# Attention, gated feed-forward and expert layer on one core: the loads of the first tiles as single steps, other tile groups, and the last block's columns split 384 and 128

## The chip, the cores and the metric

The kernel runs on one core of one Trainium2 chip. A core has five engines with an instruction stream each: TensorE (PE in the rows, with its weight loads as PEld) multiplies matrices into PSUM, VectorE (DVE), ScalarE (ACT) and GpSimd (POOL) work element by element, and SyncE (SP) issues most DMAs. The metric is the device time of one execution in microseconds, as the median of several runs. It is lower when the work ends sooner.

## The reference

```python
def _attn_ref(q, k, v):                       # q, k, v: (4, 8, 576, 64)
    scores = scale * np.matmul(q, k.transpose(0, 1, 3, 2))
    gamma = 1.0 - 2.0 ** (-5.0 - np.arange(H))
    Dmat = np.where(rel >= 0, gamma[:, None, None] ** rel, 0.0)
    return np.matmul(scores * Dmat, v)

def _moe_ref(x, w_gate, w_val, w_out, rms_g):  # x: (2304, 512), inner width 1536
    xn = x / np.sqrt(np.mean(x * x, axis=-1, keepdims=True) + 1e-06) * rms_g
    g = xn @ w_gate
    return (g / (1.0 + np.exp(-g)) * (xn @ w_val)) @ w_out

def _moe2_ref(x, w_gate, w_output_gate, w1, w2):  # 8 experts, inner width 1024
    e_idx = np.argmax(x @ w_gate, axis=1)
    ...
    for e in range(E):
        h = np.maximum(x[mask] @ w1[e], 0.0)
        out[mask] = gate_w[mask, None] * eom[mask, e, None] * (h @ w2[e])
```

The three layers follow each other: attention with decay, then a gated feed-forward layer, then one expert for each token.

## The kernel before

The 2304 tokens are 18 tiles of 128 (`TILES`, L67): tiles 0 to 3 are the first 128 positions of the four batches, and so on; tiles 16 and 17 hold two half tiles each. Float32 operands are split into a high and a low float16 half, and a product is three float16 matmuls. Attention runs tile by tile with a state per batch (`z`), in steps that have one letter each: `l` loads, `s` splits, `c` makes the scores, `o` the output with its norm, `z` the state. The four tiles of `FIRST` do it in float32: their transposed q and k come ready from memory (`qk_t`), the scores go through PSUM, are multiplied on DVE by the decay `dmat` into a tile `pp`, and `pa` is the output. From `pa` the norm goes ACT (`junk`, the sum of squares), DVE (`ss`), POOL (`rr`), DVE (`xh`), four PE transposes (`tp`), and ACT and DVE write `xt`, the input of the next layer.

The feed-forward layer takes the tiles in groups (`GROUPS`, L70: 4, 3, 3, 3, 3 and 2 tiles). For each of 12 slices `ft` of the inner width, `moe_h` (L822) makes `hg` and `hv` in PSUM (12 matmuls each, as wide as the group, in two PSUM buffers), ACT and DVE turn them into `th`, and ACT and POOL into `uh` and `ul`; `moe_out` (L854) adds their product with `wo` into an accumulator `o` for each tile. While a group is in this layer, attention of the next group's tiles runs in between. The weights come in 18 pieces of 1 MB (`load_piece`, `conv_piece`) that ACT, DVE and POOL have to decode and split (`st`, `du`, `gv_h`, `gv_l`, `wo_h`, `wo_l`); all of that lies in the first stage.

After each group `route` finds each token's expert and scatters its row. Tiles from `LATE` on go to a table of their own (80 rows for expert 0), so that expert 0 can begin with the earlier ones. `exp_l1` makes an expert's hidden layer, `exp_l2t` or `exp_l2` its output; the results go back by `yr`, an addition on POOL, a multiplication on ACT and a scattered DMA from POOL. The last expert writes by rows, and its last block of 128 tokens goes through `exp_last` (L1171).

The order on the engines isn't the order of the code. `Plan` records every operation (all show as line 232 or 294), gives each a cost (`_cost`, L328) and a due time, and a list scheduler (`schedule`, L355) writes the streams. What is recorded when in the first stage is the string `START` (L88): one word for each step, `d` loads a weight piece, `k` decodes it, `h` and `y` are pieces of `moe_h` and `moe_out`, `f` loads `dmat`, `g` loads `gain`. Until the first `moe_h` the scheduler fills every time in which its own model has TensorE idle with a matmul of zeros (`busy<-warm`, 256 columns), which computes nothing:

```python
if first in end and end[first] <= t and self.filled not in start and free.get("PE", 0.0) <= t:
    o = Op("PE", us, -1, 0)
```

How many such matmuls stand in the stream is fixed when the kernel is built. SP issues its DMAs in stream order, and a DMA that reuses one of eight semaphores waits for the one eight before it.

Of the kernel before, what the change touches and what calls it, by code (L numbers as in the profile page):

```python
# [10 lines left out]
F16 = mybir.dt.float16  # L11
# [22 lines left out]
LATE = 16  # L34
# [43 lines left out]
IN_R = 2  # L78
# [10 lines left out]
l1 d1 d0 l0 d3 s1 s0 f c1 k1 l2 k0 g c0 d12 d13 o1 o0 h0-1-0-1 k12 h0-1-1-2 h1-2-0-2 z1 s2 k3 c2 o2 e4 d2 d5 z2 k2 m  # L89
l4 d7 d8 y0-0-2 k13 z0 l3 s3 k5 h0-1-2-3 h3-4-0-2 y0-2-3 k7 c3 h1-2-2-3 h2-3-0-3 k8 s4 d4 h3-4-2-3 d6 o3 y2-1-2 k4  # L90
y3-1-3 y2-0-1 k6 d14 h2-3-3-4 h0-2-3-4 d9 y1-0-3 y2-2-3 h7-8-3-4 l5 z3 y3-0-1 h5-6-0-3 d16 k14 d15 h7-8-0-3 h4-5-0-3
y5-0-3 d10 y4-0-2 k9 e3 k15 h6-7-0-2 k16 k10 e1 c4 h6-7-2-3 d11 h8-9-3-4 o4 y4-2-3 s5 y6-2-3 e7 y6-1-2 h6-7-3-4 c5
y7-0-3 h8-10-0-3 h3-4-3-4 o5 e6 k11 h9-10-3-4 y6-0-1 l6 y8-1-3 y8-0-1 d17 h10-11-0-1 e0 e9 y9-1-2 z4 y9-0-1 s6
h11-12-0-3 y9-2-3 e8 c6 e2 h10-11-1-3 e5 h11-12-3-4 k17 o6 y10-0-2 y11-1-2 y10-2-3 y11-2-3 z6 h4-6-3-4 h10-11-3-4
y11-0-1 z5
# [146 lines left out]
class Plan:  # L242
# [85 lines left out]
    def _cost(engine, method, reads, writes):  # L328
# [175 lines left out]
def body(tc, q, k, v, qk_t, w_in, rms_g, w_route, w_exp, const, decay, empty, out):  # L504
# [85 lines left out]
    def att_load(t):  # L590
        tiles = []
        if t in FIRST:
            if t == IN_R:
                both = at.tile([P, 3, H, 2, D], F16, tag="r", name=f"l{t}", bufs=2).rearrange("p a h c d -> p (a h c d)")
            else:
                both = at.tile([P, 3, H, P], F16, tag="tr", name=f"tr{t}", bufs=2).rearrange("p a h t -> p (a h t)")
            both = both.bitcast(F32)[:, 0 : 2 * (H // 2) * P]
            sy.dma_start(out=both, in_=qk_t[t])
            tiles.append(both.rearrange("p (a b t) -> p a b t", a=2, b=H // 2))
        for nm, tag, src in (("v", "v", v), ("k", "k", k)) if t in FIRST else (("k", "k", k), ("q", "q", q), ("v", "v", v)):  # L600
            a = at2.tile([P, H, D], F32, tag=("q" if t == IN_R else tag) + "f", name=f"{nm}f{t}")
# [7 lines left out]
    split, dmat = {}, []  # L609

    def split_first(t):

        both, vf, kf = qkv.pop(t)
        split[t] = kf, (both[:, 0], both[:, 1]), vf

    def scores_first(t):
        (kt, qt), p = split[t][1], at.tile([P, 2, H, P], F16, tag="pp", name=f"pp{t}", bufs=PPB)
        probs[t] = []
        for g in range(2):
# [3 lines left out]
            with plan.group():  # L623
                for b in range(4):
                    te.matmul(ps[:, b, :], lhsT=kt[half, b, :], rhs=qt[half, b, :], start=True, stop=True)
            pf = p[:, g].rearrange("p h t -> p (h t)").bitcast(F32).rearrange("p (b t) -> p b t", t=P)
# [3 lines left out]
    def state_first(t):  # L630

        kf, _, vf = split[t]
# [13 lines left out]
    def att_split(t):  # L646
        if t in FIRST:
            return split_first(t)
# [73 lines left out]
    def att_out(t, dst):  # L722
        if t in FIRST:
            pa = pst.tile([P, H, D], F32, tag="t", name=f"pa{t}")
            vf, pf = split[t][2], probs.pop(t)
# [896 lines left out]
```

## Time and profile before

| | |
|---|---|
| median of 3 runs | 728.94 us (728.04 to 728.98) |
| the profiled execution's own time | 731.66 us |
| its span, first to last instruction | 729.4 us |
| TensorE busy in the span | 718.3 us (98%) |
| VectorE, ScalarE, GpSimd busy | 430.1, 347.2, 264.4 us |
| matmuls of zeros | 124 instructions, 17.3 us busy |
| mean granted TensorE clock | 0.998 |

The rows in the section below come from one profiled execution, in us from the start of its span. The profiled execution took 2.7 us more than the median; differences are worked out inside its span and taken from the median. A matmul's busy time includes some 0.2 us of pipeline that the next matmul overlaps, so what a matmul costs is the distance from its start to the next one's.

### The profile page before, as it was taken

Reading aid. Unit: us, or ns where it says so; the run is one execution under the profiler, and the core shown is the slowest. Engines: PE = TensorE matmul, PEld = TensorE weight load, DVE = VectorE, ACT = ScalarE, POOL = GpSimd, SP = SyncE. Lnnn points to the kernel's source line nnn. Section 1 sums busy time; section 2 is a strip of 40 time slices with the busy share of each in tenths; the row PEclk is TensorE's granted clock in tenths of the full one; section 3 lists DMA queues with packets and bytes.
Section 4 is the critical chain, followed back from the end, with each engine's and each line's share of the span. In section 5 each row is a group of like instructions: output and inputs, shape, how many; then the busy total and the mean of one; then the engine's idle time right before and its main releaser. Section 6 shows DMA issues by size and latency. Waiting matters only on the chain. (4 is left out here: it accounts for less than half of the span.)

```text
span 729.4 us, 15238 instructions
## 1 busy us (share of the span) xinstructions
PE 718.3 (98%) x6108; PEld 490.3 (67%) x6108; DVE 430.1 (59%) x918; ACT 347.2 (48%) x661; POOL 264.4 (36%) x277
## 2 busy tenths in 40 slices
PE   9999999998999999999999999999999999999996
PEld 7977667655655666566656655677876677778854
DVE  5678887738643775268526336332765774865551
ACT  3799986624532444235322234221344664765451
POOL 2576787644541443135321312131103043214115
PEclk9999999999999999999999999999999999999999
DMA  8969956671852284207322143220099899789631
GB/s 341 373 222 315 298 146 178 120 161 45 179 112 44 86 159 93 55 30 133 58 44 44 59 131 116 44 74 1 31 287 317 225 268 265 218 211 285 211 74 68
DMA packets 139673, 111.63 MB, mean 153 GB/s; under 512 B 123410, under 2 KB 123434, under 8 KB 133056
## 3 DMA queue, kind: packets, MB, share of 16 engines
q1 hardware_dynamic: 135904, 98.09, 50.9%
q0 software_dynamic: 3696, 12.54, 5.1%
q8 instruction: 49, 0.80, 0.5%
q14 instruction: 24, 0.20, 0.1%
HBM read 71.82 MB, written 14.00 MB: 118 GB/s over the span
## 5 line engine op out<-in xcount | busy, mean ns | idle before, releaser
L232 PEld LDWEIGHTS <-gv_h 128*128 128x128 f16 x1440 | 133.2, 98 | 72.2 <-issue 3.0
L232 PE MATMUL hg<-xt,gv_h 128*128 128x384 f16 (+2 forms) x624 | 134.6, 305 | 2.6 <-DVE th L232 2.6
L232 PE MATMUL hv<-xt,gv_h 128*128 128x384 f16 (+2 forms) x624 | 134.6, 305 | 0.0
L294 POOL TENSOR_TENSOR ul<-th,uh 128x384 f16<-128x384 f32 (+2 forms) x77 | 65.5, 851 | 174.4 <-ACT uh L232 173.8
L232 PEld LDWEIGHTS <-eh 128*128 128x128 f16 x1024 | 97.2, 98 | 30.5 <-issue 0.4
L232 PE MATMUL eh<-ex,eh 128*128 128x288 f16 (+7 forms) x576 | 105.1, 284 | 0.2 <-DVE hl L232 0.2
L232 PE MATMUL hv<-xt,gv_l 128*128 128x384 f16 (+2 forms) x312 | 94.2, 305 | 0.0
L232 PE MATMUL hg<-xt,gv_l 128*128 128x384 f16 (+2 forms) x312 | 94.2, 305 | 0.0
L232 DVE SCALAR_TENSOR_TENSOR th<-th,hg 128x384 f32<-128x384 f32 (+2 forms) x90 | 42.4, 471 | 85.2 <-ACT th L232 84.9
L232 DVE SCALAR_TENSOR_TENSOR el<-st,eh 128x1024 f16<-128x1024 f32 x64 | 81.6, 1303 | 17.2 <-ACT eh L294 17.2
L232 PEld LDWEIGHTS <-gv_l 128*128 128x128 f16 x720 | 70.4, 98 | 29.9
L232 ACT ACTIVATE uh<-th 128x384 f16<-128x384 f32 (+2 forms) x78 | 37.4, 481 | 106.9 <-DVE th L232 106.9
L232 PE MATMUL eh<-ex,el 128*128 128x288 f16 (+7 forms) x288 | 79.3, 284 | 0.0
L232 PE MATMUL o<-wo_h,uh 128*128 128x512 f16 x204 | 77.3, 379 | 0.0
L232 PE MATMUL o<-wo_h,ul 128*128 128x512 f16 x204 | 77.3, 379 | 0.0
L232 PE MATMUL o<-wo_l,uh 128*128 128x512 f16 x204 | 77.3, 379 | 0.0
L232 ACT ACTIVATE th<-hg 128x384 f32<-128x384 f32 (+2 forms) x90 | 38.1, 423 | 70.1 <-PE hg L232 61.9
L294 ACT ACTIVATE eh<-st 128x1024 f16<-128x1024 f32 x64 | 64.7, 1051 | 5.3 <-DMA out<-y,yx 4.4
L232 POOL TENSOR_TENSOR y<-yr 128x512 f32<-128x512 f16 x20 | 27.6, 1405 | 107.6 <-DMA yr<-yt 107.6
L232 DVE SCALAR_TENSOR_TENSOR th<-th,hv 128x384 f32<-128x384 f32 (+2 forms) x90 | 42.3, 470 | 40.2 <-PE hv L232 37.9
L232 PE MATMUL ea<-hh,eh 128*128 128x288 f16 (+5 forms) x224 | 64.9, 290 | 0.0
L232 PE MATMUL ea<-hl,eh 128*128 128x288 f16 (+5 forms) x224 | 64.9, 290 | 0.0
(194 smaller groups left out, 1222.0 us busy)
## 6 DMA issues: line engine op xcount, KB each, us to landing
st<-in_w_exp SPq DMA_DIRECT2D x32, 1024.0 KB
st<-in_w_in SPq DMA_DIRECT2D x18, 1024.0 KB
vf<-in_v SPq DMA_DIRECT2D x16, 256.0 KB
kf<-in_k SPq DMA_DIRECT2D x16, 256.0 KB
qf<-in_q SPq DMA_DIRECT2D x12, 256.0 KB
xs<-in_empty POOLq DMA_DIRECT2D x7, 385.5 KB
tr<-in_qk_t SPq DMA_DIRECT2D x3, 512.0 KB
dmat<-in_decay SPq DMA_DIRECT2D x1, 512.0 KB
```

Of the source, the lines that this page charges most:

```text
L232: return call(*map(real, args), **{a: real(b) for a, b in kw.items()})
L294: return getattr(engine, method)(*map(real, args), **{a: real(b) for a, b in kw.items()})
```

## The change

Seven things change.

- The first four tiles' loads are separate words of `START`: `l` (q and k, transposed), `v`, `a` (k by rows), `n` (the constants, which stood ahead of everything). `in_turn` chains them with the weight pieces, `dmat` and `gain`: SP issues them in the string's order. `dmat` moves to a buffer of `xt`, the score products go back into the load's own buffer (`both`, a third slot and the first) and not to `pp`, tile 3's v and k lie in `pp`.
- `START` is another string: all four first tiles' attention comes ahead of the first `moe_h`, and tile 6's attention is no longer in it.
- `GROUPS` are 4, 2, 3, 3, 3 and 3 tiles; `AHEAD` hands out attention of tiles 6 to 8 in the first two slices of the two-tile group, whose routing waits until slice 7 (`ROUTED`).
- `LATE` is 15: three tiles are late instead of two.
- The scheduler's model takes 410 GB/s for a load (330 before) and less for a short matmul.
- `exp_last` takes 384 and then 128 columns (256 and 256 before, the second half read by DVE and ACT, 128 columns each); ACT and the tile `yg` are no longer used.
- The second to last expert's three additions `y<-yr` are on DVE instead of POOL.

```diff
-LATE = 16
+LATE = 15
-GROUPS = [[0, 1, 2, 3]] + [[3 * _g + 1, 3 * _g + 2, 3 * _g + 3] for _g in range(1, 5)] + [[16, 17]]
+GROUPS = [[0, 1, 2, 3], [4, 5]] + [[3 * _g, 3 * _g + 1, 3 * _g + 2] for _g in range(2, 6)]
-AHEAD = [[2] * NF, [2] * NF]
+AHEAD = [[8, 7] + [0] * (NF - 2), [2] * NF]
+ROUTED = 7
-l1 d1 d0 l0 d3 s1 s0 f c1 k1 l2 k0 g c0 d12 d13 o1 o0 h0-1-0-1 k12 h0-1-1-2 h1-2-0-2 z1 s2 k3 c2 o2 e4 d2 d5 z2 k2 m
+g l0 l1 f c0 n v0 v1 d0 v2 l2 o0 d1 l3 d12 a1 v3 k0 k1 c1 a0 c2 o1 c3 o2 o3 k12 a3 z1 h1-2-0-3 d2 h0-1-0-3 k2 z0
...
-            return writes[0].free / 2400 + (0.0025 if writes[0].free > 200 else 0.008), False, 0.0
+            return max(writes[0].free / 2400 + 0.0026, 0.025), False, 0.0
-            rate = 174e3 if method == "dma_start_transpose" else 330e3
+            rate = 174e3 if method == "dma_start_transpose" else 410e3
...
     def att_load(t):
+        if t in FIRST:
+            both = at.tile([P, 3, H // 2, P], F32, tag="r" if t in IN_R else "tr", name=f"l{t}", bufs=2)
+            in_turn(sy.dma_start(out=both[:, 0:2].rearrange("p a b t -> p (a b t)"), in_=qk_t[t]))
+            split[t] = both
+            return
...
+    def in_turn(o):
+
+        if turn_of:
+            o.order.add(turn_of[-1])
+        turn_of.append(o)
+        return o
...
     def scores_first(t):
-        (kt, qt), p = split[t][1], at.tile([P, 2, H, P], F16, tag="pp", name=f"pp{t}", bufs=PPB)
+        both = split.pop(t)
...
-            pf = p[:, g].rearrange("p h t -> p (h t)").bitcast(F32).rearrange("p (b t) -> p b t", t=P)
+            pf = both[:, (2, 0)[g]]
...
-        for c0 in (0, DM // 2):
-            c = slice(c0, c0 + DM // 2)
+        for c in (slice(0, DM - P), slice(DM - P, DM)):
             exp_l2(w, hh, hl, a, r0, n, 0, NEF, c)
-            for i in range(1 + (c0 > 0)):
-                k = DM // 2 // (1 + (c0 > 0))
-                c = slice(c0 + i * k, c0 + i * k + k)
-                if i:
-                    ac.activation(y[:n, c], a[:n, c], AF.Copy, scale=g[:n])
-                else:
-                    ve.tensor_scalar(out=y[:n, c], in0=a[:n, c], scalar1=gate, scalar2=1.0 / S_W, op0=ALU.mult, op1=ALU.mult)
+            ve.tensor_scalar(out=y[:n, c], in0=a[:n, c], scalar1=gate, scalar2=1.0 / S_W, op0=ALU.mult, op1=ALU.mult)
...
-            po.tensor_tensor(out=y, in0=yr[:, 0, :, j], in1=yr[:, 1, :, j], op=ALU.add)
+            adder.tensor_tensor(out=y, in0=yr[:, 0, :, j], in1=yr[:, 1, :, j], op=ALU.add)
...
-                if waiting:
+                if waiting and ft >= (ROUTED if g == 1 else 0):
```

The start of SP's stream before (`st` is a weight piece, `tr` and `l` the transposed q and k, `vf` and `kf` v and k by rows, numbers count buffers):

```order
L232 DMA cst<-in_const 128x526
L232 DMA st<-in_w_in 128x1024
L232 DMA tr_128<-in_qk_t 128x1024
L232 DMA st<-in_w_in 128x1024
L232 DMA dmat<-in_decay 128x1024
L232 DMA tr_198<-in_qk_t 128x1024
L232 DMA vf_209<-in_v 128x512
L232 DMA vf_218<-in_v 128x512
L232 DMA gain<-in_rms_g 128x512
L232 DMA st<-in_w_in 128x1024 x2
```

and the same stretch of SP's stream now:

```order
L233 DMA gain<-in_rms_g 128x512
L233 DMA l_107<-in_qk_t 128x1024
L233 DMA l_116<-in_qk_t 128x1024
L233 DMA dmat<-in_decay 128x1024
L233 DMA cst<-in_const 128x526
L233 DMA vf_141<-in_v 128x512
L233 DMA vf_146<-in_v 128x512
L233 DMA st<-in_w_in 128x1024
L233 DMA vf_171<-in_v 128x512
L233 DMA l_175<-in_qk_t 128x1024
L233 DMA st<-in_w_in 128x1024
```

Two weight pieces of 1 MB stood second and fourth; now six loads of attention and `cst` stand ahead of the first piece.

TensorE's stream at the first scores before, behind 51 matmuls of zeros:

```order
L232 MATMUL busy<-warm 128x256
L232 MATMUL sc_0_193<-tr_128 128x128 x4
L232 MATMUL sc_1_202<-tr_128 128x128 x4
L232 LDWEIGHTS warm
L232 MATMUL busy<-warm 128x256
```

and now, behind 19 of them:

```order
L233 MATMUL busy<-warm 128x256
L233 MATMUL sc_0_156<-l_107 128x128 x4
L233 MATMUL sc_1_161<-l_107 128x128 x4
L233 MATMUL sc_0_166<-l_116 128x128 x4
L233 LDWEIGHTS warm
L233 MATMUL busy<-warm 128x256
```

The first scores moved up by 32 matmuls of zeros. In the whole stream there are 124 of these before and 85 now: 19, 3, 20, 2, 1, 14, 4, 15 and 7, with work of the first four tiles between them.

DVE's stream in the first group behind the start, where a tile's output and the splits of another one's q and k (`r`) meet `th`. Before, in a group of three tiles:

```order
L232 TENSOR_TENSOR pa_2696<-pa_2696,cst 128x512
L232 TENSOR_TENSOR z_149<-kv_2753,z_149 128x512
L232 SCALAR_TENSOR_TENSOR r_2776<-kf_2298,r_2776 128x8x64
L232 TENSOR_TENSOR pa_2696<-pa_2696,gain 128x512
L232 TENSOR_SCALAR ss_2794<-ss_2794 128x1
L232 SCALAR_TENSOR_TENSOR r_2776<-qf_2323,r_2776 128x8x64
L232 SCALAR_TENSOR_TENSOR th<-th,hg 128x384
L232 SCALAR_TENSOR_TENSOR th<-th,hv 128x384
```

and now, in the group of two:

```order
L233 TENSOR_TENSOR pa_2185<-pa_2185,cst 128x512
L233 TENSOR_TENSOR z_138<-kv_2245,z_138 128x512
L233 TENSOR_TENSOR pa_2185<-pa_2185,gain 128x512
L233 TENSOR_SCALAR ss_2262<-ss_2262 128x1
L233 SCALAR_TENSOR_TENSOR r_2269<-qf_1512,r_2269 128x8x64
L233 SCALAR_TENSOR_TENSOR r_2269<-kf_1536,r_2269 128x8x64
L233 SCALAR_TENSOR_TENSOR xh_2308<-pa_2185,rr_2297,xh_2308 128x512
L233 SCALAR_TENSOR_TENSOR th<-th,hg 128x256
```

The same operations stand ahead of a `th`, which is 256 columns wide now, with `xh` ahead of it too.

## Rows read from the trace of the kernel before

**Rows 1.** The page, first part: busy us (share of the span) xinstructions.

```profile
PE 718.3 (98%) x6108; PEld 490.3 (67%) x6108; DVE 430.1 (59%) x918; ACT 347.2 (48%) x661; POOL 264.4 (36%) x277
```

**Rows 2.** Waits of PE: who waited for whom, us in total, times, longest.

```profile
PE hg L232 <- DVE th L232: 2.6, 1, 2.6
PE busy L232 <- DVE warm L232: 1.0, 1, 1.0
PE sc L232 <- DVE xh L232: 0.6, 1, 0.6
PE xr L232 <- ACT x L294: 0.5, 1, 0.5
```

**Rows 3.** Timeline of PE at the start: start, length, operation.

```profile
1.03 8.64 PE L232 MATMUL busy<-warm 128*128 128x256 f16 x51 [1.03 <-DVE warm L232]
9.60 1.71 PE L232 MATMUL sc<-tr 64*128 64x128 f32 x16
11.24 4.65 PE L232 MATMUL busy<-warm 128*128 128x256 f16 x41
15.82 1.16 PE L232 MATMUL sc<-tr 64*128 64x128 f32 x8
16.91 2.00 PE L232 MATMUL pa<-vf,pp 128*128 128x64 f32 x16
18.84 1.16 PE L232 MATMUL sc<-tr 64*128 64x128 f32 x8
...
22.54 0.60 PE L232 MATMUL tp<-identf,xh 128*128 128x128 f32 x4
22.98 2.56 PE L232 MATMUL busy<-warm 128*128 128x256 f16 x22
...
26.07 1.15 PE L232 MATMUL kv<-vf,kf 128*64 128x64 f32 x16
27.14 0.39 PE L232 MATMUL busy<-warm 128*128 128x256 f16 x2
27.47 1.16 PE L232 MATMUL sc<-l 64*128 64x128 f32 x8
28.55 0.29 PE L232 MATMUL hg<-xt,gv_h 128*128 128x128 f16 x2
```

**Rows 4.** Stretches: zero matmuls' busy time (x), granted clock, DMA share, GB/s.

```profile
1.00:5.00 4.00, 3.97 (x19) 1.00 0.81 280
5.00:7.00 2.00, 2.00 (x12) 1.00 1.03 420
7.00:9.60 2.60, 2.60 (x24) 1.00 0.97 410
```

**Rows 5.** Timeline of the first tile's norm.

```profile
18.94 0.60 ACT L232 ACTIVATE junk<-pa 128x512 f16<-128x512 f32 x1 [3.69 <-PE pa L232]
...
20.64 0.74 DVE L232 SCALAR_TENSOR_TENSOR xh<-pa,rr,gain 128x512 f32<-128x512 f32 x1
```

**Rows 6.** One stretch, all engines: PE, PEld, DVE, ACT, POOL busy (x).

```profile
28.55:100.00 71.45, 70.73 (x727) 53.57 (x727) 59.66 (x116) 65.87 (x120) 51.01 (x48) 1.00 0.81 269
```

**Rows 7.** Timeline around the longest wait of PE.

```profile
176.95 4.69 DVE L232 SCALAR_TENSOR_TENSOR r<-qf,r 128x512 f16<-128x512 f32 x1
...
177.28 1.05 POOL L232 TENSOR_TENSOR z<-z,cst 128x512 f32<-128x512 f32 x1
...
179.95 1.14 POOL L294 TENSOR_TENSOR zl<-z,zh 128x512 f16<-128x512 f32 x1
```

**Rows 8.** Timeline of the end.

```profile
723.26 0.27 PE L232 MATMUL ea<-eh,hl 128*128 128x256 f16 x1
723.57 0.35 DVE L232 TENSOR_SCALAR ys<-ea,em 128x128 f32<-128x128 f32 x1 [1.87 <-PE ea L232]
724.00 0.37 ACT L232 ACTIVATE ys<-ea,yg 128x128 f32<-128x128 f32 x1 [8.23 <-DVE ys L232]
724.65 0.97 POOL L1193 DMA_INDIRECT out<-ys,yx  x1 [1.70 <-DVEq L1572]
```

More of the change, by code (lines that the diff above doesn't have):

```diff
@@ L590, in att_load @@
     def att_load(t):
-        tiles = []
-        if t in FIRST:
-            if t == IN_R:
-                both = at.tile([P, 3, H, 2, D], F16, tag="r", name=f"l{t}", bufs=2).rearrange("p a h c d -> p (a h c d)")
-            else:
[L596 to L601, printed above, removed]
+        if t in FIRST:
[3 more added lines that the diff above has]
+            return
+        tiles = []
+        for nm, src in (("k", k), ("q", q), ("v", v)):
+            a = at2.tile([P, H, D], F32, tag=nm + "f", name=f"{nm}f{t}")
             o = 0
@@ L607, in att_load, with load_first @@
         qkv[t] = tiles
[L609 to L614, printed above, removed]
+    split, dmat, vf_first, kf_first, lone, turn_of = {}, [], {}, {}, [], []
+    def in_turn(o):
[3 more added lines that the diff above has]
+        return o
+    def load_first(t, nm, src, to):
+        if t == LONE:
+            if not lone:
+                lone.append(at.tile([P, 2, H, D], F32, tag="pp", name=f"kv{t}", bufs=PPB))
+            a = lone[0][:, int(nm == "k")]
+        else:
+            a = at2.tile([P, H, D], F32, tag=("q" if t in IN_R else nm) + "f", name=f"{nm}f{t}")
+        b, s0, n = TILES[t][0]
+        in_turn(sy.dma_start(out=a.rearrange("p h d -> p (h d)"), in_=src[b * S + s0 : b * S + s0 + n]))
+        to[t] = a
     def scores_first(t):
-        (kt, qt), p = split[t][1], at.tile([P, 2, H, P], F16, tag="pp", name=f"pp{t}", bufs=PPB)
+        both = split.pop(t)
         probs[t] = []
@@ L1335, in overflow_block @@
         exp_store(mp, a, xr[:, DM : DM + 2], P, False)
-    sy.dma_start(out=cst, in_=const)
     ve.memset(warm, 0.0)
@@ L1344, in body @@
     ve.memset(mhalf, -0.5)
-    ve.tensor_tensor(
-        out=identf, in0=cst[:, C_MASK : C_MASK + P], in1=cst[:, C_TRI : C_TRI + P], op=ALU.subtract
-    )
     xg = {}
@@ L1396, in hidden, with expert @@
         return [pl.tile([P, NEF, width], F16, tag=nm, name=nm) for nm in ("hh", "hl")]
-    def expert(pl, w, x, mt, cap, by_rows, done=None, aside=()):
+    def expert(pl, w, x, mt, cap, by_rows, done=None, aside=(), adder=po):
         hh, hl = done or hidden(pl)
@@ L1455, in start @@
             elif step == "f":
-                dm = (
-                    at.tile([P, 3, H, 2, D], F16, tag="r", name="dmat", bufs=2)
-                    .rearrange("p a h c d -> p (a h c d)").bitcast(F32)[:, 0 : H * P]
-                )
-                sy.dma_start(out=dm, in_=decay)
-                dmat.append(dm.rearrange("p (h t) -> p h t", t=P))
-            elif step == "g":
-                sy.dma_start(out=gain, in_=rms_g.unsqueeze(0).to_broadcast([P, DM]))
+                dmat.append(xp.tile([P, H, P], F32, tag="xt", name="dmat"))
+                in_turn(sy.dma_start(out=dmat[0].rearrange("p h t -> p (h t)"), in_=decay))
+            elif step == "g":
+                in_turn(sy.dma_start(out=gain, in_=rms_g.unsqueeze(0).to_broadcast([P, DM])))
+            elif step[0] == "n":
+                in_turn(sy.dma_start(out=cst, in_=const))
+                ve.tensor_tensor(
+                    out=identf, in0=cst[:, C_MASK : C_MASK + P], in1=cst[:, C_TRI : C_TRI + P], op=ALU.subtract
+                )
+            elif step[0] == "v":
+                load_first(i, "v", v, vf_first)
+            elif step[0] == "a":
+                load_first(i, "k", k, kf_first)
             elif step[0] == "d":
@@ L1565, in body @@
             fetch(i + 1)
-        expert(mp, wts[i], *gat.pop(i), RANKED[ORDER[i]], last)
+        expert(mp, wts[i], *gat.pop(i), RANKED[ORDER[i]], last, adder=ve if i == E - 3 else po)
         if i == 0:
```

27 lines of the change are left out of this document (11 added, 16 removed).

## The prediction

> **What bounds the kernel now.** I read the page first: PE is busy 98% of the span and the other four far less [rows 1], so the sum of what PE is given sets the end. Then the waits of PE: beside the first 1.0 us there are only 2.6, 0.6 and 0.5 us in the whole run [rows 2]. So three things can move the time: PE work that computes nothing, PE's few waits, and what follows the last matmul. The timeline of the start shows the first kind: 51, 41, 22, 2 and (between rows left out) 8 matmuls of zeros, 124 in all, between the first useful work [rows 3]. The first 51 last from 1.03 to 9.60, 8.57 us. The 41 behind the first scores last from 11.24 to 15.82, 0.112 us each, and at that price the other 73 take 8.2 us. Together they are 16.8 us. Their pace has two levels: 19 in the first 4 us, 24 in the 2.6 us up to 9.60 [rows 4]. That is 1.2 and then 2.4 GHz, though the clock column reads 1.00 in all three rows; PE had done nothing but zeros from 1.03 on when the pace rose, near 7 us. Of the second kind, the longest wait has a cause in sight [rows 7]; of the third, the last rows show one step after the other [rows 8].
>
> **The change part by part.** *Matmuls of zeros.* 85 remain. The first 19 come at the slow pace: 4 us for 19 [rows 4]. The other 66 cost 0.112 each [rows 3], 7.4 us. That is 11.4 instead of 16.8: **-5.4 us**, if nothing else fills the room.
>
> *The slow pace meets useful work.* The zeros end at about 5.1 us, and PE's clock rose near 7. What runs in between is now the first scores, in place of zeros: 1.9 us at half pace, which loses 0.95 us: **+0.95**. It is nothing if the first scores begin only at 7, and then a wait of 1.9 stands there; so 0.5 to 1.9.
>
> *The loads.* The queue moved 280 GB/s from 1 to 5 us, then 420 and 410 [rows 4]: 1.1 MB by 5.0, 2.0 by 7.0, 3.0 by 9.6. `gain` and tile 0's q and k are 0.79 MB, so they are there by 5; `gain` however is one row copied to all partitions, of unknown price at this place, and I allow 0.5 us (0 to 1.5): **+0.5**. Everything later has room: `dmat` (1.84 MB) near 6.7, `cst` and tile 0's v (2.4 MB) near 8.0, while PE reaches tile 0's output only behind four score groups, past 10.
>
> *The norm chain.* From the end of `pa` (18.84, where the next work starts [rows 3]) to the end of `xh` (20.64 + 0.74 [rows 5]) is 2.5 us. Behind tile 0's output stand 20 zeros, 2.2 us, so `tp` waits 0.3. Behind tile 2's stand a `tp` (0.44), a `pa` (1.93) and 4 zeros (0.45) [rows 3], 2.8 us: covered, unless ACT comes late with `junk`, since decoding now stands among these steps on ACT. **+0.4** in all (0 to 2).
>
> So the start gives -5.4 + 0.95 + 0.5 + 0.4 = **-3.5 us** (-4.9 to 0). As a check, the first `hg` should start near 34 us: 1.0 of idle time, 11.4 of zeros, 1.9 for the three items, and useful work of eight score groups (1.64 for two, 1.09 for a single one: about 8), four `pa` (7.7), four `tp` (1.8) and two `kv` (2.1). It started at 28.55 with five, two, two and one of these done.
>
> *Weights.* The first piece stood behind `cst`, at 1.3 MB of the queue; now it ends at 3.7 MB. By the same rates that is 11.2 us instead of 5.5, so decoding starts 5.7 us later. Its user, the first `hg`, starts 5.4 us later as well, and tile 6's splits have left this stage. So 0, but the cover is thin: ACT was busy 65.87 of 71.45 us behind the first `hg` [rows 6]. Uncovered it costs up to 5.7.
>
> *Groups.* The same columns go through `moe_h` and `moe_out` in fewer, wider pieces: 0. Three last tiles bring eight more transposes of 128 columns to PE; no row has one that alone, and with nothing below and a 256-column matmul at 0.112 above I take half: **+0.45** (0 to 0.9). Their rows, `early` and the ranks come a tile later; the first expert's 256 rows are ready then and hide it, as they did. The 0.5 us wait of `xr` [rows 2] may go or stay.
>
> *The end.* ACT started at 724.00, after DVE, took 0.37, and POOL's store came 0.28 later [rows 8]. Without ACT's step the store follows DVE's end (723.92) by the same 0.28: 724.20 instead of 724.65, **-0.45** (-0.5 to 0). The columns before it are the same. The three additions moved to DVE stand behind its last `hl`; nothing on PE waits for them: 0.
>
> *Waits behind the start* were 3.7 us [rows 2]. Their places all move. I take the same sum, **0**, with -3.7 and +6.6 (below) as ends.
>
> The sum is -3.5 + 0.45 - 0.45 = -3.5 us. Inside the profiled span that is 729.4 to 725.9; the profiled run was above the median, so I take it from the median: 728.94 - 3.5 = **725.4 us**.
>
> **The rivals.** *DVE jams in the two-tile group: slower.* The 2.6 us wait came from one DVE instruction, the split of q, that stayed 4.69 us, from 176.95 to 181.64, while POOL ran from 177.28 to 181.09 without a pause [rows 7]; `th`, and behind it `hg`, had to wait. The Trainium skill has this on its GPSIMD Engine Reference, Specifications: GpSimd shares its SBUF interfaces with VectorE, and instructions with two SBUF inputs contend. The row agrees in kind: q and its high half are two SBUF inputs. By rows, the mechanism here is this. One slice of a two-tile group is 24 matmuls at 0.112 and 6 of twice the width, 4.0 us; one of three tiles is 6.0 us. A hold of the same length then costs 2.0 us more, 4.6. Three tiles are split in that group. One such hold would take 2.0 us of the gain (727.4); from the second on the kernel is slower: two are 9.2 less the 2.6 that was there before, 725.4 + 6.6 = 732.0. Against it: DVE's load a slice falls with the width too, and one hold that long stands in the whole trace before.
>
> *Weights come late: slower.* The 5.7 us of later decoding reach PE: 725.4 + 5.7 = 731.1. For it speaks ACT's 92% [rows 6]; against it that PE had no wait for a weight [rows 2], and that the first use moves as far as the load.
>
> *The start does not get shorter: the same.* PE waits where zeros stood: the loads or the norm chains take 3.5 us more than I allow, the first `hg` comes past 37, and the time is 728.9. For it: four norm chains through four engines now stand ahead of the first `hg`, and every wait there is on the path. Against it: 66 zeros remain in between as cover.
>
> *The waits go: faster still.* None of the start's waits and none of the later 3.7: 725.4 - 0.9 - 3.7 = 720.8.
>
> **How the numbers follow.** The forecast has a chance of 0.50, the further gain 0.14, no shorter start 0.16, the jam 0.13, late weights 0.07. A measurement of this kernel can tell about 0.2%, 1.5 us, from no change. Faster by more than that: 0.64, the first two. The same: 0.16. Slower: 0.20. The range reaches from 721.0, near the further gain, to 731.0, the case of late weights, with the jam's upper half left out. The predicted time is the forecast's, 725.4.
>
> **What would show it.** Right: the zeros' busy time falls to 11 or 12 us, the first `hg` stands between 33 and 35 us with all four first tiles' outputs ahead of it, PE's waits add up to 3 to 5 us, and no ACT step stands between the last DVE one and the last store. Wrong at the start: PE rows with idle time that ended by a load or by `xh` before 34 us. Wrong later: `hg` or `hv` waiting for `th` around 130 to 190 us (the jam), or for `gv_h` or `gv_l` between 35 and 100 us (late weights).

## The result: slower, and the profile after

The changed kernel takes **733.34 us** (median of 6 runs, 731.08 to 737.52), the kernel before 728.47 beside it: a ratio of 1.0073, 95% interval 1.0044 to 1.0101. The prediction was 725.4 (721.0 to 731.0), so it has the sign and the range wrong. The profiled execution took 733.03 us, with a span of 730.9.

The first part of the page of the changed kernel, its busy times, and its row of the granted TensorE clock in 40 slices:

```profile
PE 718.0 (98%) x5957; PEld 483.0 (66%) x5957; DVE 432.3 (59%) x913; ACT 344.1 (47%) x649; POOL 262.2 (36%) x269
...
PEclk7999999999999999999999999999999999999999
```

TensorE runs 151 instructions fewer than in [rows 1] and is busy just as long. The first slice of the clock says why. The same in stretches of the start (us from the span's start; busy time of PE, PEld, DVE, ACT and POOL with instructions; granted clock; DMA share; GB/s):

```profile
1.00:5.50 4.50, 4.24 (x19) 2.70 (x19) 1.62 (x5) 1.00 (x1) 1.62 (x4) 1.00 0.50 183
5.50:8.90 3.40, 1.98 (x22) 1.99 (x23) 0.00 (x0) 0.00 (x0) 0.00 (x0) 1.00 1.00 399
8.90:19.10 10.20, 10.20 (x48) 8.35 (x47) 4.59 (x11) 2.22 (x4) 1.57 (x2) 0.50 1.03 421
19.10:28.00 8.90, 8.67 (x75) 7.58 (x73) 6.48 (x12) 5.51 (x8) 3.35 (x3) 1.00 1.00 400
```

From 8.9 to 19.1 us the granted clock is 0.50, that is 1.2 GHz, and TensorE is busy all the time. (The first row reads 1.00 at half pace, as in [rows 4]: 19 zeros take 4.24 us.) The timeline of PE shows the same stretch (start, length, operation; in brackets the idle time before it and what ended it):

```profile
1.03 4.24 PE L233 MATMUL busy<-warm 128*128 128x256 f16 x19 [1.03 <-DVE warm L233]
6.92 2.76 PE L233 MATMUL sc<-l 64*128 64x128 f32 x24 [1.65 <-DMA l<-in_qk_t]
9.61 0.82 PE L233 MATMUL busy<-warm 128*128 128x256 f16 x3
10.36 2.07 PE L233 MATMUL sc<-l 64*128 64x128 f32 x8
12.37 3.67 PE L233 MATMUL pa<-vf,l 128*128 128x64 f32 x16
15.83 3.96 PE L233 MATMUL busy<-warm 128*128 128x256 f16 x20
19.63 0.60 PE L233 MATMUL tp<-identf,xh 128*128 128x128 f32 x4
...
38.95 0.48 PE L233 MATMUL hg<-xt,gv_h 128*128 128x384 f16 x2
```

Against [rows 3]: the zeros end at 5.27 as planned, then TensorE stands still for 1.65 us until tile 0's q and k have landed. Most of the first 24 score passes still run at full pace (2.69 us to the next start). Then everything takes about twice as long: `pa` 3.67 us instead of 2.00, 20 zeros 3.96 where 22 took 2.56. The first `hg` starts at 38.95.

The waits of PE (who waited for whom, us in total, times, longest):

```profile
PE hg L233 <- DVE th L233: 2.4, 4, 0.9
PE sc L233 <- DMA l<-in_qk_t: 1.6, 1, 1.6
PE busy L233 <- DVE warm L233: 1.0, 1, 1.0
PE eh L233 <- DVE hl L233: 0.7, 1, 0.7
PE xr L233 <- ACT x L295: 0.5, 1, 0.5
PE sc L233 <- DMA tr<-r: 0.5, 1, 0.5
```

The one wait of 2.6 us for `th` in [rows 2] is gone; four shorter ones, near 62 and 110 us, have come. The end, for [rows 8] (the last matmul, the last VectorE step, the last store):

```profile
725.15 0.22 PE L233 MATMUL ea<-eh,hl 128*128 128x128 f16 x1
725.41 0.35 DVE L233 TENSOR_SCALAR ys<-ea,em 128x128 f32<-128x128 f32 x1 [0.82 <-PE ea L233]
726.14 0.97 POOL L1193 DMA_INDIRECT out<-ys,yx  x1 [0.30 <-DVE ys L233]
```

The store starts 0.99 us after the last matmul, against 1.39 before.

### The profile page after: what moved, and what is told of

It reads as the page before. It is cut to its first block, busy times and chain, and to the rows that moved or that the text cites. A ratio compares the mean times of both kernels' runs of the same rounds, so it can differ in the third digit from the quotient of the medians.

```text
span 730.9 us, 14905 instructions
## 1 busy us (share of the span) xinstructions
PE 718.0 (98%) x5957; PEld 483.0 (66%) x5957; DVE 432.3 (59%) x913; ACT 344.1 (47%) x649; POOL 262.2 (36%) x269
## 5 line engine op out<-in xcount | busy, mean ns | idle before, releaser
L233 PEld LDWEIGHTS <-gv_h 128*128 128x128 f16 x1360 | 127.1, 98 | 75.2 <-issue 3.3
L233 PE MATMUL hg<-xt,gv_h 128*128 128x384 f16 (+1 forms) x584 | 133.6, 315 | 1.7 <-DVE th L233 1.5
L233 PE MATMUL hv<-xt,gv_h 128*128 128x384 f16 (+1 forms) x584 | 133.6, 315 | 0.0
L233 DVE SCALAR_TENSOR_TENSOR el<-st,eh 128x1024 f16<-128x1024 f32 x64 | 83.4, 1331 | 18.0 <-ACT eh L295 16.3
L233 PE MATMUL hv<-xt,gv_l 128*128 128x384 f16 (+1 forms) x292 | 91.8, 315 | 0.0
L233 PE MATMUL hg<-xt,gv_l 128*128 128x384 f16 (+1 forms) x292 | 91.8, 315 | 0.0
L233 PEld LDWEIGHTS <-gv_l 128*128 128x128 f16 x680 | 66.5, 98 | 31.8
L233 PE MATMUL ea<-hh,el 128*128 128x288 f16 (+5 forms) x224 | 64.9, 290 | 0.0
```

The costliest lines, as they stand in the source:

```text
L233: return call(*map(real, args), **{a: real(b) for a, b in kw.items()})
```

## The experiments

The runs were made on five chips. The kernel before takes 728.0 to 728.5 us on some of them and 731.8 to 732.0 on others, so every ratio is to the kernel before on the same chip. "Set A" are the chips with 728, "set B" those with 732. The result above is one of 728.

| run | edit | us | before | ratio (95%) |
|---|---|---|---|---|
| e1 | after, 16 more zeros first | 730.32 | 728.28 A | 1.0033 (1.0021 to 1.0044) |
| e2 | after, `gain` loaded later | 730.09 | 728.28 A | 1.0032 (1.0013 to 1.0052) |
| e3 | before, first zeros 51 to 19 | 730.68 | 728.28 A | 1.0030 (1.002 to 1.004) |
| e4 | after, 16 more zeros behind the scores | 733.25 | 728.28 A | 1.0061 (1.0044 to 1.0078) |
| e5 | e1 with the clears behind | 733.12 | 731.80 B | 1.0014 (1.0 to 1.0029) |
| e6 | before, new end | 732.54 | 731.80 B | 1.0006 (0.9995 to 1.0017) |
| e7 | before, first zeros 51 to 35 | 729.82 | 731.80 B | 0.9980 (0.9965 to 0.9996) |
| e8 | after, 12 more zeros first | 730.89 | 731.80 B | 0.9998 (0.9973 to 1.0022) |
| e9 | after, weight pieces first, zeros moved | 737.17 | 731.91 B | 1.0078 (1.0063 to 1.0094) |
| e10 | before, new groups | 728.40 | 731.91 B | 0.9954 (0.994 to 0.9968) |
| e11 | e7, second zeros 41 to 25 | 731.56 | 731.91 B | 0.9995 (0.9981 to 1.0009) |
| e12 | after, again | 735.50 | 731.91 B | 1.0051 (1.0026 to 1.0077) |
| e13 | e10 and e7 | 728.00 | 731.99 B | 0.9948 (0.9934 to 0.9961) |
| e14 | e1, 40 more zeros before `hg` | 735.81 | 731.99 B | 1.0050 (1.0035 to 1.0066) |
| e15 | after, old groups | 752.01 | 731.99 B | 1.0275 (1.0242 to 1.0307) |
| e16 | e1, again | 730.91 | 727.98 A | 1.0033 (1.002 to 1.0046) |
| e17 | e1, `th` ahead of `st` once | 730.20 | 727.98 A | 1.0031 (1.0017 to 1.0045) |
| e18 | e13, again | 727.15 | 731.84 B | 0.9937 (0.9923 to 0.995) |

e5 to e12 ran on one chip, e1 to e4 on another; e13 to e15 shared a third, e16 and e17 a fourth.

### The clock at the start

**e1 and e16: more zeros ahead of the first scores.** In both, and in most of the others, a few lines behind the scheduler change the length of a run of zeros and nothing else. The diff is the same each time with other numbers (`{0: 16}`: run 0 gets 16 more, and a negative number takes the last ones away):

```diff
+ZEROS = {0: 16}
-            for o in self.schedule():
+            order, runs, last = self.schedule(), [], None
...
+            for r, more in ZEROS.items():
+                for o in runs[r][len(runs[r]) + more :] if more < 0 else ():
+                    order.remove(o)
+                at = order.index(runs[r][-1]) + 1 if more > 0 else 0
+                order[at:at] = [runs[r][-1]] * max(more, 0)
+            for o in order:
```

Expected of e1:

> The changed kernel with 16 more matmuls of zeros behind the first 19, so that TensorE has work until tile 0's q and k are there. Theory A (the stretch of 10.24 us at half clock follows from the 1.65 us in which TensorE stood still before its first scores): no such stretch, granted clock 0.998; the scores start near 8.0 us instead of 6.92, which costs 1.1, and the half pace gives back 4.8: 733.3 - 3.7 = 729.6 us. Theory B (the float32 scores that now come so early bring the clock down, not the pause): the stretch stays, granted clock near 0.992, time 734.4 us. Theory C (the clock changes by chance from run to run and has nothing to do with the start): granted clocks scattered between 0.988 and 0.997 as before, time near 734.

Of e16:

> The changed kernel with 16 more zeros in the first run, once more, to stand beside the next kernel on the same chip. Theory A: full clock (0.997 or more) in most runs, a ratio of 0.999 to 1.001 where the kernel before takes 731.9 and 1.003 where it takes 728.3; hg's waits for th 2.4 us or more in the profile.

The granted clock is 0.996 or more in 15 of the 16 runs of this kernel (0.989 in the other, the profiled execution of e1). It was 0.988 to 0.997 in all ten runs of the changed kernel, those of e12 with them. The timeline of PE at the start of e16:

```profile
1.03 5.87 PE L234 MATMUL busy<-warm 128*128 128x256 f16 x35 [1.03 <-DVE warm L234]
6.90 2.45 PE L234 MATMUL sc<-l 64*128 64x128 f32 x24
9.28 0.50 PE L234 MATMUL busy<-warm 128*128 128x256 f16 x3
10.27 1.16 PE L234 MATMUL sc<-l 64*128 64x128 f32 x8 [0.49 <-DVE l L234]
11.36 2.00 PE L234 MATMUL pa<-vf,l 128*128 128x64 f32 x16
...
35.30 0.48 PE L234 MATMUL hg<-xt,gv_h 128*128 128x384 f16 x2
```

The scores start at the same 6.90, since the 16 zeros fill the pause. With the pace kept, the first `hg` starts 3.65 us earlier, and the time is 2.4 to 3.0 us lower (733.34 to 730.32 and 730.91). For this stretch theory A holds, theory C falls, and B falls as it was put: the scores come as early and the clock stays. What A leaves is a kernel that is still 1.0033 in set A; the longest waits in e16's trace are 3.7 us of `hg` for `th`, as expected, and 1.9 us of `sc` for `xh`.

The low execution of e1 shows a fall of another kind. Its first scores keep full pace, but from 20.3 to 27.1 us the granted clock is 0.52:

```profile
19.07 2.82 PE L234 MATMUL pa<-vf,l 128*128 128x64 f32 x16 [0.23 <-DVE l L234]
...
24.04 3.06 PE L234 MATMUL busy<-warm 128*128 128x256 f16 x14
```

The changed kernel's trace has 1.70 us for the same 14 zeros. Ahead of it TensorE waited only 0.4 us twice and 0.2 us once. So a pause as long as 1.65 us is not always there when the clock falls; what brought it down here stays open.

**e8: 12 more zeros.**

```diff
+ZEROS = {0: 12}
```

> The changed kernel with 12 more matmuls of zeros at the start instead of 16: 31 in all, which end at 7.0 to 7.2 us, where tile 0's q and k land. Theory A: the pause is 0.2 us or none, full clock (0.998) in nearly all runs, 0.45 us less than with 16: 729.9 us. If the number of zeros at full pace is what decides, not the pause, more of the runs show 0.990 to 0.996 than with 16, and the median is 731 to 733 us.

Eight of ten runs show 0.997 or more, two 0.987 and 738 us. 0.9998 here against 1.0051 of the changed kernel on the same chip: filling the pause and keeping the clock up is worth some 3.9 us there, with about 2 us of uncertainty in each of the two ratios. The profiled execution is one of the two low ones: it is at half clock from 20.9 to 38.0 us, behind waits of 0.2 to 0.6 us. So 12 or 16 zeros make a fall rare and do not exclude it.

**e2: no pause, but scores at 5.1 us.**

```diff
-g l0 l1 f c0 n v0 v1 d0 v2 l2 o0 ...
+l0 l1 f c0 n v0 v1 g d0 v2 l2 o0 ...
```

> The changed kernel with the load of the gain row (one row copied to all partitions) moved behind tile 1's v instead of ahead of everything. The same 16 to 19 zeros stand first. Tile 0's q and k should be there by about 4 us, so TensorE does not stand still before the first scores (1.65 us less). Theory A (the pause brings the clock down): no half-clock stretch, 733.3 - 1.65 - 4.8 = 726.8 us. Theory B (the early float32 scores do it): the stretch stays, 731.7 us. Theory C (chance): scattered clocks, about 731. If the row load is not what delays tile 0's q and k, the pause stays at 1.6 us and the time at 733.

The pause is gone, so the row load of `gain` was what delayed tile 0's q and k. But the timeline of PE shows that the clock did not rise:

```profile
1.03 4.02 PE L233 MATMUL busy<-warm 128*128 128x256 f16 x18 [1.03 <-DVE warm L233]
5.14 5.46 PE L233 MATMUL sc<-l 64*128 64x128 f32 x32
10.53 3.67 PE L233 MATMUL pa<-vf,l 128*128 128x64 f32 x16
13.99 3.98 PE L233 MATMUL busy<-warm 128*128 128x256 f16 x20
17.81 0.60 PE L233 MATMUL tp<-identf,xh 128*128 128x128 f32 x4
```

The stretch of the scores and `pa` in the columns of the result's stretches:

```profile
5.10:14.00 8.90, 8.86 (x49) 8.64 (x50) 3.22 (x8) 0.00 (x0) 0.00 (x0) 1.00 1.02 371
```

`pa` takes 3.46 us to the next start (1.93 at full pace [rows 3]), the score passes before it are as slow, and the pace doubles only among the last of the 20 zeros. From 5.1 to 14 us TensorE was busy 8.86 of 8.9 us. So A is too narrow and B has a part: float32 scores and outputs that began at 1.2 GHz stayed at it in this trace, and the clock rose among the zeros behind them. The clock column reads 1.00 here, and 0.999 for the whole execution; only the pace shows the half clock. The ten runs read 0.986 to 0.999. The first `hg` starts at 37.03, and the time falls by some 3 us.

**e4: the same 16 zeros behind the scores.**

```diff
+ZEROS = {1: 16}
```

> The changed kernel with 16 more matmuls of zeros, not ahead of the first scores but behind the first three score groups, where 3 stand; the pause of 1.65 us before the scores stays. Theory A: half clock as in the changed kernel, and 16 zeros at 0.213 us more, less what the waits behind them give back: 735 to 737 us, granted clock 0.992. Theory B (too little work of the scores' kind, not the pause): zeros behind them keep the clock up, 0.997 or more, 730 to 731 us. Theory C: scattered clocks, about 735.

The stretches of e4, in the columns of the first such block:

```profile
5.20:8.70 3.50, 1.86 (x21) 1.79 (x21) 0.00 (x0) 0.00 (x0) 0.00 (x0) 1.00 1.02 405
8.70:12.10 3.40, 3.40 (x17) 2.51 (x17) 1.89 (x3) 0.00 (x0) 0.00 (x0) 0.50 1.04 422
12.10:24.00 11.90, 11.29 (x97) 9.84 (x95) 6.62 (x14) 4.97 (x8) 2.04 (x3) 1.00 1.03 410
```

The clock falls behind the pause, at 8.7, as in the changed kernel, but is up again at 12.1, among the zeros that stand there; in the changed kernel, with `pa` in that place, it came back 7 us later. The zeros cost about what they bring: 733.25, not the 735 to 737 of theory A. The trace also has half clock from 111 to 114.5 us, behind a wait of 1.9 us for `th`.

**e3: the same pause in the kernel before**, whose first run loses its last 32 zeros.

```diff
+ZEROS = {0: -32}
```

> The kernel before, with the first 51 matmuls of zeros cut to 19; nothing else is changed. Its first q and k land near 7.2 us, so TensorE stands still from 5.1 to about 7.4 and the scores come 2.2 us earlier than before. Theory A (a pause brings the clock down for 10.24 us): half clock from about 10 to 20 us, granted clock near 0.992, and the time is 728.5 - 2.2 + 5.0 = 731.3 us at most, less where what follows was waiting anyway. Theory C (chance, or something else in the change): full clock, 726.3 to 728.5 us. Theory B says half clock here as well.

TensorE waits 2.76 us for its first load, and then:

```profile
4.20:7.60 3.40, 0.64 (x7) 0.33 (x4) 0.06 (x1) 1.32 (x2) 0.00 (x0) 1.00 1.00 407
7.60:14.40 6.80, 6.80 (x34) 5.48 (x35) 5.21 (x8) 3.75 (x5) 1.64 (x1) 0.50 0.99 370
```

A kernel with 32 zeros fewer and nothing else changed runs 6.8 us at half clock and ends 2.4 us later. The fall needs neither the new order nor the new groups.

### Each part alone

**e10: the new groups with the old start.** LATE, GROUPS, AHEAD and ROUTED as in the change, and tile 6's five words taken out of the old `START`.

```diff
-LATE = 16
+LATE = 15
+GROUPS = [[0, 1, 2, 3], [4, 5]] + [[3 * _g, 3 * _g + 1, 3 * _g + 2] for _g in range(2, 6)]
+AHEAD = [[8, 7] + [0] * (NF - 2), [2] * NF]
+ROUTED = 7
...
```

> The kernel before, with its start as it was, and only the groups of the changed kernel: 4, 2, 3, 3, 3, 3 tiles, LATE 15, its AHEAD and ROUTED, and tile 6's attention taken out of the first stage. By the prediction's terms: +0.45 us for eight more transposes and 0 for the rest, ratio 1.0006. Rival (VectorE jams in the two-tile group, where three tiles are split during two slices): hg waits 2 us and more for th there, ratio 1.003 to 1.009. If tile 6's absence from the first stage frees ScalarE there and waits go: 0.998.

All that the view of PE's waits lists in this trace:

```profile
PE busy L233 <- DVE warm L233: 1.0, 1, 1.0
PE sc L233 <- DVE xh L233: 0.6, 1, 0.6
PE xr L233 <- ACT x L295: 0.5, 1, 0.5
```

-3.5 us on a chip of set B: the wait of 2.6 us of [rows 2] is gone and nothing has come for it. VectorE does not jam in the two-tile group; that rival falls. What the other 0.9 us are is not shown. In this trace the same 51 zeros end at 8.77 us and not at 9.60 [rows 3], which the groups cannot have caused, so the traces do not settle it.

**e12: the whole change on the same chip**, with no edit.

> The changed kernel as it is, once more, beside the same runs of the kernel before as the three others, since the kernel before took 728.3 us in one set of runs and 731.8 in another. Theory A: granted clocks of 0.988 to 0.997 again and a ratio of 1.004 to 1.010 if the kernel before is at 728; near 1.002 if it is at 731.8, where the kernel before has a wait of 2.7 us that the other set does not show.

735.5 against 728.4 of the groups alone: what is left of the change costs 7.1 us. Most of it should be the new start, since the new end brings nothing (e6); the additions on VectorE and the scheduler's new rates have no run of their own. By the ratios 3.9 us of it are the clock and the pause (e8) and 3.2 remain, both give or take 2 us.

**e15: the new start with the old groups.**

```diff
-LATE = 15
+LATE = 16
+GROUPS = [[0, 1, 2, 3]] + [[3 * _g + 1, 3 * _g + 2, 3 * _g + 3] for _g in range(1, 5)] + [[16, 17]]
-ROUTED = 7
+AHEAD = [[2] * NF, [2] * NF]
+ROUTED = 0
```

> The changed kernel with the old groups of 4, 3, 3, 3, 3 and 2 tiles, LATE 16 and the old hand-out of attention; tile 6's attention, which the new start no longer has, comes at the end of the first stage. If start and groups add up: 1.0051 + 0.0046 = 1.0097 beside the kernel before, with the half-clock stretch of about 10 us at the start and hg's waits near 60 and 110 us as in the changed kernel. If the new start is slow only together with the new groups: 1.003 or less. Tile 6's steps at the end of the stage may add a wait of their own there.

20 us slower, with new waits between 153 and 167 us, the longest 8.3 us of `lg` for `x<-rt`, where the first stage ends with tile 6's attention. It prices nothing but that misfit; that start and groups simply add is not shown by it.

**e6: the new end alone**, `exp_last` as in the change:

```diff
-        for c0 in (0, DM // 2):
+        for c in (slice(0, DM - P), slice(DM - P, DM)):
```

> The kernel before with the new exp_last alone (384 and then 128 columns, all on VectorE). By the prediction's term: -0.45 us (728.3 to 727.85), the last store follows VectorE's last step directly. Against it: in the changed kernel one matmul of the last 128 columns waits 0.24 us for VectorE's ys; then it is -0.2 us. If the end is worth nothing the time stays at 728.3.

No gain. The last matmul, VectorE step and store of e6:

```profile
723.81 0.22 PE L232 MATMUL ea<-eh,hl 128*128 128x128 f16 x1
724.97 0.35 DVE L232 TENSOR_SCALAR ys<-ea,em 128x128 f32<-128x128 f32 x1 [1.72 <-PE ea L232]
725.60 0.97 POOL L1184 DMA_INDIRECT out<-ys,yx  x1 [1.11 <-DVE ys L232]
```

VectorE starts 1.16 us after the last matmul, in the trace of the changed kernel 0.26, in the kernel before 0.31. What delays it in one execution and not in another stays open. It is more than the 0.45 us that the prediction gave for the step of ScalarE.

### What the new start costs beside the clock

**e5: the clears of the tables behind the weights** (on top of e1): the ten words of `START` stand together near its end.

```diff
-h3-4-3-4 e6 m h4-5-0-1 d6 e2 y3-0-1 ...
+h3-4-3-4 m h4-5-0-1 d6 y3-0-1 ...
...
+... h10-11-0-3 e6 e2 e0 e1 e5 e4 e3 e8 e7 e9 k17
```

> The changed kernel with 16 more matmuls of zeros at the start (730.3 us with these alone) and, beside that, the ten words that clear the expert tables (e0 to e9, 0.8 MB and less each) recorded at the end of the first stage instead of in its first half. Theory D (what is left of the loss, 2.0 us against the kernel before, comes from weight pieces that land late while the DMA engines are 93% busy: ScalarE waits for a piece with th queued behind it, and TensorE's hg then waits for th near 60 and 110 us): ScalarE's waits for weight pieces fall from 2.9 us or more to under 1.5, hg's waits for th from 2.4 to 5.4 us to under 1, and the time to 728.3 to 729.0 us. Theory E (these waits come from VectorE's own load, not from the pieces): hg's waits and the time stay, 730.3 us. If the clears are then missing where rows are scattered, a new wait stands behind 140 us and the time is above 731.

ScalarE's waits for pieces are 3.4 us (8.2 in e16), `hg` and `hv` wait 3.6 us for `th`, and a wait of 1.4 for `tr<-r` has come. The time is not below that of e8, on the same chip. The clears are not the cause.

**e9: weight pieces earlier.**

```diff
-g l0 l1 f c0 n v0 v1 d0 v2 l2 o0 d1 l3 d12 a1 v3 ...
+l0 l1 d0 f c0 n v0 v1 d1 g v2 l2 o0 l3 d12 a1 v3 ...
...
+ZEROS = {0: 16, 1: -15, 3: -4, 5: -5, 8: -16}
```

> The changed kernel with 34 matmuls of zeros in the first run (so the clock should stay up, about 730.3 us where the kernel before has 728.3), and with the first two weight pieces moved up in the chain of loads: the first directly behind the q and k of tiles 0 and 1, the second behind the v of tiles 0 and 1, the gain row behind it. The zeros in the later runs number 63, against 66. Theory D (the weight pieces come too late, ScalarE waits for one with th queued behind it, and TensorE waits for th near 60 and 110 us): decoding starts 2 to 4 us earlier, hg's waits for th fall from 2.4 to 5.4 us to under 1.5, and the ratio to the kernel before falls by 0.002 to 0.003 against the one with 16 more zeros (1.0033 there). Theory G (the pieces are paced by the five load buffers and by decoding, whenever the first one lands): the waits stay at 2 us or more, ratio as with 16 more zeros.

Worse: `hg` waits 4.3 us for `th`, ScalarE 12.9 for pieces, and the clock is at half for 3.4 us from 13.1. The scheduler also placed other steps anew, and the zeros stand elsewhere, so this shows only that earlier pieces alone do not help.

**e14: 40 zeros ahead of the first `hg`.**

```diff
+ZEROS = {0: 16, 8: 40}
```

> The changed kernel with 16 more zeros in the first run and 40 more in the last one, directly ahead of the first hg: TensorE begins the weights' users 4.5 us later, while loading and decoding go on. Theory D (the weights are decoded too late against the first hg): hg's waits for th near 60 and 110 us fall from 2.4 to 5.4 us to under 0.5, and the time is 4.5 us less 2 to 4 us above the one with 16 zeros alone, a ratio of 1.004 to 1.006 beside it as 1.000 to 1.003. Theory H (the order in which decoding, splits and th stand on ScalarE and VectorE makes the waits, however late the first hg is): the waits stay at 2 us or more, ratio 1.006 to 1.010.

The first two rows of the waits of PE:

```profile
PE hg L234 <- DVE th L234: 5.0, 4, 2.5
PE busy L234 <- DVE warm L234: 1.0, 1, 1.0
```

With 4.5 us more for loading and decoding, the waits are longer, not gone, and beside e8 in set B the kernel is slower by 0.0052, 3.8 us, nearly the zeros. The waits speak against theory D and for H: they come with the order, however late the first `hg` is. The time does not decide, since 1.0050 lies in the range of D.

**e17: one exchange in ScalarE's stream.** At the one place where the decoding step `st` stands directly ahead of a `th`, the two are exchanged:

```diff
+            for st in [o for o in order if o.kind == "st"]:
+                a = order.index(st)
+                b = next((i for i, o in enumerate(order[a + 1 :], a + 1) if o.engine == "ACT"), a)
+                if order[b].kind == "th" and not any(st in o.after | o.order for o in order[a:b]):
+                    order.insert(b, order.pop(a))
```

> The same kernel with one exchange in ScalarE's stream: the th of 128 columns near 61 us stands ahead of the decoding step st that it stood behind; st waits there for its piece of weights. Theory H (st waits for a load with th queued behind it, and hg waits for that th): hg's wait of 0.85 to 3.0 us near 60 us is gone, the waits near 110 us stay, and the time is 0.9 to 2.5 us below the kernel without the exchange. If VectorE's own steps are what th waits for, the wait near 60 us stays and the time does not move. If the piece is late anyway and its user is next, a wait for gv_h or gv_l takes the place of the one removed and the time does not move.

The place in the timeline of all engines:

```profile
57.08 1.41 DVE L234 SCALAR_TENSOR_TENSOR st<-du,st 128x512 int32<-128x512 int32 x2
...
57.34 0.28 ACT L234 ACTIVATE th<-hg 128x128 f32<-128x128 f32 x1 [0.68 <-PE hg L234]
...
57.51 1.15 ACT L234 ACTIVATE st<-st 128x1024 int32<-128x1024 uint32 x1
...
58.41 0.28 DVE L234 SCALAR_TENSOR_TENSOR th<-th,hg 128x128 f32<-128x128 f32 x1
...
58.74 0.48 PE L234 MATMUL hg<-xt,gv_h 128*128 128x384 f16 x2 [0.69 <-DVE th L234]
```

ScalarE is done with `th` at 57.6 now, but VectorE takes it up at 58.41, behind two decoding steps of a piece. So the wait of 0.7 us is VectorE's order, as the second case of the expectation has it; time as e16 within the intervals. Near 110 us the changed kernel shows the like with a split: `r<-kf` of 2.05 us, `pa` and `st` ahead of `th`. There it is read, not tested. So the 2 us that remain in set A look like such waits, by their place in the streams; no run here removes them.

### A version that beats both

**e7 and e11: fewer zeros in the kernel before.** e7 cuts the first run to about where the load lands.

```diff
+ZEROS = {0: -16}
```

> The kernel before with the first 51 matmuls of zeros cut to 35, so that they end near 7.6 us, when tile 1's q and k have just landed (7.57 us was the start of the scores with 19 zeros) and the clock has risen. Theory A (the clock comes down where TensorE stands still early, not because zeros are fewer): granted clock stays at 0.998, the scores start at 7.7 instead of 9.6, and the time is 728.3 - 1.8 = 726.5 us if the rest can follow, 728.3 if loads, norms or weights were late by as much. If fewer zeros alone bring the clock down: 0.995, 730 to 731 us, as with 19.

-2.0 us, clock 0.996 to 0.999. In its trace `sc` waits 0.7 us for the load and no half clock follows. e11 cuts the second run as well (`ZEROS = {0: -16, 1: -16}`):

> The kernel before with its first two runs of zeros cut, 51 to 35 and 41 to 25. The first cut alone gave a ratio of 0.998 (-2.0 us). If zeros at full pace are simply time: another 16 x 0.112 = 1.8 us, ratio 0.9955. If the load of tile 0's q and k (landed at 12.2 us before) or the norms are then late, TensorE stands still in their place: 0.998. If such a pause among float32 scores brings the clock down: 1.000 or more, granted clock 0.996 or less.

Nothing more is gained: short waits for a load and `xh` (0.4 and 0.3 us) stand where the zeros stood, and after its wait of 2.6 us for `th` the clock is at half for 3.4 us.

**e13 and e18: the new groups and 35 zeros first**, the edits of e10 and e7 together.

> The kernel before with the new groups alone (ratio 0.9954) and the first run of zeros cut from 51 to 35 (0.998 by itself). If the two add: 0.9934, near 727 us where the kernel before takes 731.9, and a little over 724 where it takes 728.3; granted clock 0.997 or more. If the groups gain only by removing a wait of 2.7 us near 181 that the kernel before shows in one set of runs and not in the other: 0.998 where it takes 728.3. If weights are late for the earlier first hg: 0.9954, the cut brings nothing.

> The new groups and the first run of zeros cut to 35, once more. If the kernel before takes 728 us beside it: ratio 0.994 to 0.996 if the groups gain in themselves, 0.997 to 0.999 if their gain was only the wait of 2.7 us that the kernel before has in the other set of runs (the cut alone is worth 1 to 2 us). If the kernel before takes 732 us: 0.9948 again, and the question stays open.

728.00 and 727.15 us where the kernel before takes 732 and the changed kernel 735.5: the fastest of all in set B. That the cut adds to the groups is not shown: 0.9948 and 0.9937 stand between the 0.9954 of the groups alone and the 0.9934 of a full sum, and the intervals overlap. Set A did not come up for it, so whether the groups gain on such a chip stays open.

## Why the prediction was wrong

**Slow pace and loads, the step that failed.** The prediction priced the slow pace at 0.95 us (0.5 to 1.9), as something that ends near 7 us by itself. The trace: full pace by 6.92, then 10.2 us at half clock, a loss of 5.1. The load of `gain` was given 0.5 us (0 to 1.5); the wait was 1.65, where before there was none [rows 3]. These two are 5.3 us more than allowed, and the first `hg` stands at 38.95 where 33.9 was worked out: 5.05 late. In e1 and e16, 16 more zeros kept the pace at this place in most executions and gave 2.4 to 3.0 us back. The view that could have warned is [rows 4]: the row from 1 to 5 us gives the clock as 1.00 while the pace is half, so "the clock rose near 7" said when it rises under zeros and nothing on when it falls. The Trainium skill's TensorE: Matmul & The Clock Gate, section HAM oscillation — how this bites in real kernels, tells of a matmul loop whose waits for the next load sent the clock down, so that each next tile started cold; the trace agrees in kind, with 10.2 us at half clock. It differs in size: the section's waits are 3 to 5 us, and here the clock fell after 1.65 us of waiting, with most of 24 score passes at full pace in between. The prediction did not weigh it.

**The time it was taken from.** The profiled execution of before stood 2.7 us above its median, and the prediction took its difference from the median, 728.94. But that execution holds the wait of 2.6 us, which not all runs have. Its 731.66 us lie above all 48 runs of that kernel in set A (727.4 to 730.0) and among those of set B (730.5 to 733.7); on which chip it ran is not on record. On set B three more traces of that code (e6, e7, e11) show it with the same 4.7 us of `r<-qf,r` [rows 7]. In e3, of set A, the same instruction looks like this, beside GpSimd:

```profile
179.29 1.00 POOL L1025 DMA_INDIRECT xs<-rt,ix  x1 [0.28 <-POOL rt L1022]
...
179.56 0.68 DVE L233 SCALAR_TENSOR_TENSOR r<-qf,r 128x512 f16<-128x512 f32 x1
180.33 1.05 POOL L233 TENSOR_TENSOR z<-z,cst 128x512 f32<-128x512 f32 x1
```

VectorE is through before GpSimd's four steps begin, and the split takes 0.68 us. In the slow case GpSimd begins 0.33 us after the split [rows 7], here 0.77 us after it. That this is what parts the two sets is likely from these five traces, not shown. A trace of one sort and a median of the other were compared: 2.7 us, and with the 5.05 that is 7.75 of the 7.94 us missed.

**Matmuls of zeros.** 85 remain, as said. They are busy 14.7 us, not 11 to 12: behind the first 19, some 18 more ran at half pace, about 0.1 us each too long, and the rest is pipeline at the ends of the nine runs, which busy time counts. The count was right and the price was not.

**Norm chains.** 0.4 us was allowed; a wait of 0.2 for `xh` stands there, beside 0.2 for `l`, a score product. Right.

**Weights.** "0, but the cover is thin": no matmul of the changed kernel waits for a weight. Right for the weights. What decoding does instead, at the one place tested, is to stand ahead of `th` on VectorE (e17). That term was looked for on ScalarE.

**Groups, and waits behind the start.** The sum of the waits was kept at 0, with ends of -3.7 and +6.6. It came out by luck, of two parts: the groups take the 2.6 us wait away (e10), the new start brings 2.4 us for `th` back. Behind the first `hg` the changed execution takes 691.95 us, the one before 700.85: 8.9 less, which is what the prediction's terms make (3.55 us less in all, and a first `hg` 5.35 us later). No run separates the 0.45 us for the transposes.

**The end.** -0.45; 0.40 in the trace of the changed kernel, no gain in e6. **The adds** on VectorE: no wait of PE names them.

**The rivals.** "The start does not get shorter" came nearest, by its sign "first `hg` past 37", but it had loads or norm chains in mind and 3.5 us, not the clock. The jam in the two-tile group and late weights did not come.

## What to carry over

A matmul of zeros is not only filler: at the start of this kernel it kept the clock up for the work that follows in most executions. So cut such a run to about where the first load lands, and look at the granted clock of the stretch behind it, and at the pace too, since the clock column read 1.00 at half pace in e2. Compare a profiled execution with a median only after asking whether its longest waits are in the other runs. A change of several parts can hide a good one: here, on the chips of set B, the groups alone gain 3.5 us and the rest of the change loses twice that.

## What was not expected of the hardware

In e2 TensorE ran 8.9 us of float32 scores and outputs without a gap at 1.2 GHz, and the rise to 2.4 GHz came among the 20 zeros behind them. When the clock rises under the same zeros differs from run to run: 35 of them took 5.87 us in e16 and 6.59 in e1.

A wait in the middle of dense float16 work can be followed by half clock too. After the 2.6 us wait of e6, which ends at 180.9 us:

```profile
181.70:185.10 3.40, 3.40 (x20) 2.19 (x19) 0.55 (x2) 0.82 (x2) 0.91 (x1) 0.50 1.00 186
185.10:190.00 4.90, 4.90 (x73) 3.41 (x72) 3.40 (x6) 1.72 (x3) 1.04 (x1) 1.00 0.88 187
```

3.4 us at half clock follow, that is 1.7 us more. e11 shows it after the same wait, the kernel before and e7 don't: the price of a wait differs from run to run.

A row copied to all partitions (`gain`, 256 KB) at the head of the queue held back the load behind it: with `gain` later, the first scores started at 5.14 us and not at 6.92 (e2). The queue moved 183 GB/s up to 5.5 us and 399 after, against 280 at the start of the kernel before [rows 4]; without `gain` at its head it moved 225 up to 5.5 us (e2), so the row explains a part of the slow start and not all of it.
